# First-block weights of a linear-attention kernel: from a TensorE gram to VectorE row sums, from the second batch on

## The chip, the cores and the metric

The kernel runs on one core of a Trainium2 chip. A core has TensorE (matrix products, with a separate path that loads the stationary operand), VectorE, ScalarE, GpSimd, and SyncE, whose queue issues nearly all DMAs here. In the profile's rows they are PE, PEld, DVE, ACT, POOL and SP. The metric is the device time of one execution in microseconds; shown are medians over several runs, and one further execution is profiled.

## The reference

Two blocks follow each other. The first is a linear attention with a decaying state (B, H, S, D = 4, 8, 768, 48; everything float32); the second is an MLP mixer over tokens and then over channels (model width 384, hidden widths 256 and 1536).

```python
for t in range(S):
    cur = np.einsum('bhd,bhe->bhde', u[None] * kt, vt)
    y[:, :, t] = np.einsum('bhd,bhde->bhe', rt, state + cur)
    state = wt[:, :, :, None] * state + np.einsum('bhd,bhe->bhde', kt, vt)
# x = y with the heads side by side: (B, S, 384)
xt = x.transpose(0, 2, 1)
h = np.maximum(xt @ w_tok1, 0.0) @ w_tok2
u = x + h.transpose(0, 2, 1)
out = u + np.maximum(u @ w_ch1, 0.0) @ w_ch2
```

Written as weights, token t sees an earlier token s with weight sum over d of r[t,d] k[s,d] times the decays w between them. It sees itself with sum over d of r[t,d] u[d] k[t,d], and the token right before it with sum over d of r[t,d] k[t-1,d], with no decay.

## The kernel before

The attention is worked in twelve units: unit i covers 256 tokens of one batch (`NU = 12`, three units to a batch, `UB = 3`), as two chunks of 128 tokens (`UC = 2`) and four pairs of heads (`A = 4`). r, k and w lie with head dimension on partitions and tokens along the row, in three rotating sets of buffers (`rs`, `ks`, `ws`), so unit i uses set i % 3. The weights inside a block of 64 tokens are gathered in `weights_at[i % 3]`, a tile of 128 partitions by 1024.

`levels(i)` makes these weights by doubling block sizes. `begin` (L214) makes on ScalarE two helper copies, `rp` and `kp`, in which r and k of neighbouring tokens are mixed with u, and `first_block` (L325) multiplies the first decays into r and k (`join`, three VectorE products), forms a gram of `kp` and `rp` on TensorE for each chunk (`gram0`, L242, 64 matrix products of the profile's count per unit) and copies the 2 by 2 blocks on the diagonal of it into the weights (`pick0`, L248, two predicated copies on VectorE). Levels 1 to 5 then each run one gram (L265, for level 5 L259), one `join` (L297 to L299) and one `pick` (VectorE's predicated copy L281 for levels 1 to 3, ScalarE copies L276 and L289 for levels 4 and 5). A level's gram reads r and k as the join of the level before left them, and its own join has to wait until the gram has read them.

`post(i)` uses the weights: `tokens` transposes k (L331, copied by ScalarE at L332), `carry` multiplies it with v (L341), `update` advances the state on VectorE (L358, a chain over chunks), `before` multiplies r with the state (L378), `within` multiplies the weights with v (L391), and ScalarE copies the result into x. At its end the loads of unit i + 3 are issued from SyncE.

`mixing(bt)` is the MLP of a batch: `hidden` (L429), `back` (L436, whose result VectorE adds to x at L438), `turn` (transposes L448), `up` (L456, ScalarE applies the relu at L458), and the second channel product, which for all but the first 256 tokens is done in `quarters` as seven half-size products (L490) in place of eight. The seven results are read from PSUM by ScalarE (L499) or VectorE (L500 to L528) and summed; VectorE also makes three sums of z beforehand (L482 to L485). Their PSUM tiles and those of `up`, `hidden` and `back` share two buffers (`ps_m`), so a product can start only when the product two before it has been read. The grams, the transposed k and some `turn`s share two other buffers (`ps_g`).

The order of the work: the attention of batch 0 runs at the start, woven with the conversion of the mixer's weights, which VectorE makes from 64-bit input. From then on `woven` lays the attention pieces of the following batch (units 3 to 5 beside batch 0's mixer, 6 to 8 beside batch 1's, 9 to 11 beside batch 2's) between the pieces of the mixer, by given costs. `beside` couples unit i's `post` with unit i + 1's `levels`, so that two groups of small products stand next to each other. The framework schedules inside these pieces: it decides the final order of each engine's queue from the dependencies and its own estimates, and each queue then runs strictly in that order.

Lines of the profile that matter below: L226 and L230 (rp, kp on ScalarE), L242, L248, L265, L281, L297 to L299, L358, L438, L482 to L485, L490, L500 to L528.

## Time and profile before

| what | value |
|---|---|
| median of 5 runs | 613.35 us (610.61 to 614.23) |
| profiled execution | 614.57 us, of it the span of the trace 612.9 us |
| TensorE matrix products busy | 584.3 us, 95% of the span |
| TensorE weight loads busy | 498.1 us, 81% |
| VectorE busy | 341.2 us, 56% |
| ScalarE busy | 201.6 us, 33% |
| moved by DMA | 38.63 MB, mean 63 GB/s |

A row of the page's groups reads: line, engine, operation, tile written <- tiles read, shapes and count, then the busy time in us, the mean ns of one, and the idle time of the engine just before the group with what ended most of it. The timeline gives start, duration, engine, line, operation and count, with idle time in front in brackets. Matrix products overlap, so a duration is longer than the distance from one start to the next; the same holds to a lesser degree on VectorE (a 0.69 us product is followed by the next start after 0.61 us).

### The profile page before, as it was taken

The numbers are of one execution on the slowest core, as the hardware profiler recorded it, in microseconds if no ns is written. First come the engines' busy times: TensorE is split into PE (matmuls) and PEld (weight loads), VectorE is DVE, ScalarE is ACT, GpSimd is POOL, SyncE is SP. The second block draws the span as 40 slices with busy tenths as digits, with TensorE's granted clock in tenths as the row PEclk, the third lists the DMA queues.
The fourth block names the chain that finished last, engine by engine and source line by source line (L and its number), as shares of the span: only waits on it lengthen the run. The fifth ranks groups of instructions, "written<-read, shape, count | busy, mean of one in ns | idle before, by whom it ended". The sixth has DMA issues, their size and how long they took to land.

```text
span 612.9 us, 19865 instructions
## 1 busy us (share of the span) xinstructions
PE 584.3 (95%) x8980; PEld 498.1 (81%) x8980; DVE 341.2 (56%) x743; ACT 201.6 (33%) x500; POOL 7.2 (1%) x32
## 2 busy tenths in 40 slices
PE   2889789999999999999999999999999999999997
PEld 2777567876988886789899896789899895898987
DVE  5889789998676783636464472516254431040403
ACT  6154555530445433432332422332212411302020
POOL 4000000000000000000000000000000000000000
PEclk9999679999999999999999999999999999999999
DMA  8336564620232212111112100000000000000000
GB/s 346 112 81 215 150 175 157 214 84 27 55 107 80 55 55 79 28 49 32 54 28 79 27 29 27 2 2 3 27 2 28 2 17 11 1 14 14 27 1 26
DMA packets 19380, 38.63 MB, mean 63 GB/s; under 512 B 2112, under 2 KB 12864, under 8 KB 19296
## 3 DMA queue, kind: packets, MB, share of 16 engines
q1 hardware_dynamic: 19152, 37.36, 19.3%
q8 instruction: 70, 1.15, 0.8%
q14 instruction: 14, 0.11, 0.1%
q10 hardware_dynamic: 144, 0.00, 0.0%
HBM read 32.64 MB, written 4.72 MB: 61 GB/s over the span
## 4 chain that ended last, share of the span: by engine, by line
PE 86%; DVE 7%; ACT 3%; issue 2%; DMA 2%; SPq 0%; ACTq 0%; DVEq 0%
PE z_ps L456 28%; PE q_ps L490 24%; PE gram L265 8%; PE h_ps L429 6%; PE h_ps L436 5%; PE h_ps L466 3%; PE y_ps L391 2%; PE kv_ps L341 2%; PE gram L331 2%; PE y_ps L378 2%; PE xT_ps L448 1%; PE gram L242 1%; PE gram L259 1%; DMA scratch<-in_w_ch_dram 1%; DVE state L358 1%
## 5 line engine op out<-in xcount | busy, mean ns | idle before, releaser
L456 PE MATMUL z_ps<-xT,wch 128*128 128x256 f32 x864 | 196.1, 382 | 0.1
L456 PEld LDWEIGHTS z_ps<-xT,wch 128*128 128x128 f32 x864 | 160.9, 190 | 22.1 <-ACT z L458 1.0
L458 ACT ACTIVATE z<-z_ps 128x256 f32<-128x256 f32 x144 | 55.0, 382 | 149.3 <-PE z_ps L456 140.3
L490 PE MATMUL q_ps<-wch,z 128*128 128x192 f32 x528 | 94.8, 329 | 0.0
L490 PEld LDWEIGHTS q_ps<-wch,z 128*128 128x128 f32 x528 | 86.1, 190 | 1.4
L265 PEld LDWEIGHTS gram<-r,k 48*64 48x64 f32 x3072 | 60.5, 156 | 12.6 <-issue 7.2
L490 PE MATMUL q_ps<-scratch,z 128*128 128x192 f32 x396 | 70.6, 329 | 0.0
L265 PE MATMUL gram<-r,k 48*64 48x32 f32 x3072 | 65.6, 237 | 4.7 <-issue 1.9
L490 PEld LDWEIGHTS q_ps<-scratch,z 128*128 128x128 f32 x396 | 64.4, 190 | 0.5
L297 DVE TENSOR_TENSOR k<-k,decay 112x512 f32<-112x512 f32 x36 | 24.8, 690 | 47.3 <-PE gram L265 35.4
L482 DVE TENSOR_TENSOR z<-z 128x768 f32<-128x768 f32 x11 | 10.5, 957 | 60.4 <-ACT z L458 60.4
L297 DVE TENSOR_TENSOR k<-k,w 112x512 f32<-112x512 f32 x36 | 24.8, 689 | 34.6 <-PE gram L265 29.0
L358 DVE SCALAR_TENSOR_TENSOR state<-state,w_chunk,kv_ps 128x48 f32<-128x48 f32 x160 | 30.8, 257 | 21.2 <-PE kv_ps L341 21.1
L429 PE MATMUL h_ps<-x,wtok 128*128 128x384 f32 x96 | 39.8, 562 | 1.7 <-ACT x L397 1.6
L436 PE MATMUL h_ps<-h,wtok 128*128 128x384 f32 x96 | 35.5, 493 | 0.1
L438 DVE TENSOR_TENSOR x<-x,h_ps 128x384 f32<-128x384 f32 x24 | 13.3, 554 | 36.6 <-PE h_ps L436 36.1
L281 DVE COPY_PREDICATED at<-mask,gram 128x512 f32<-128x512 uint8 x36 | 32.3, 898 | 0.0
L429 PEld LDWEIGHTS h_ps<-x,wtok 128*128 128x128 f32 x96 | 19.9, 219 | 13.2 <-issue 3.0
L289 ACT COPY at<-gram 16x256 f32<-16x256 f32 x48 | 17.4, 363 | 38.6 <-PE gram L265 37.4
L242 PE MATMUL gram<-rp,kp 48*64 48x64 f32 x768 | 18.0, 245 | 10.9 <-ACT kp L230 7.9
L298 DVE TENSOR_TENSOR r<-r,w 112x512 f32<-112x512 f32 x36 | 24.6, 685 | 4.8 <-ACT rp L226 4.8
L242 PEld LDWEIGHTS gram<-rp,kp 48*64 48x64 f32 x768 | 15.9, 154 | 12.7 <-ACT kp L230 10.7
(77 smaller groups left out, 554.5 us busy)
## 6 DMA issues: line engine op xcount, KB each, us to landing
scratch<-in_w_ch_dram SPq DMA_DIRECT2D x10, 512.0 KB, 4.5
vt<-in_v_dram SPq DMA_DIRECT2D x12, 384.0 KB, 3.5
out_dram<-o SPq DMA_DIRECT2D x24, 192.0 KB, 1.9
x<-in_w_ch_dram SPq DMA_DIRECT2D x8, 512.0 KB, 4.5
w<-in_rkw_dram SPq DMA_DIRECT2D x18, 192.0 KB, 3.6
k<-in_rkw_dram SPq DMA_DIRECT2D x18, 192.0 KB, 3.1
r<-in_rkw_dram SPq DMA_DIRECT2D x18, 192.0 KB, 3.7
scratch<-in_w_tok_dram SPq DMA_DIRECT2D x4, 512.0 KB, 9.1
```

Of the source, the lines that this page charges most:

```text
L242: pe.matmul(g[cols, q, ts(a, T)], L["kp"][rows, tokens], L["rp"][rows, tokens], start=True, stop=True)
L265: fours(lambda q, j, rows, cols: pe.matmul(g[cols, q, ts(ca, 32)], k_[rows, ds(ca * 128 + j * T, T)], right[rows, ts(2 * ca + j, 32 // b), ...
L281: dve.copy_predicated(out=dst, data=g.rearrange("p q (m b) -> p q m b", b=b), mask=masks[l].rearrange("p x t -> p (x t)").rearrange("p (m ...
L297: dve.tensor_mul(left, left, wv[:, :, 1].unsqueeze(2).to_broadcast([ROWS, n, b]))
L298: dve.tensor_mul(right, right, wv[:, :, 0].unsqueeze(2).to_broadcast([ROWS, n, b]))
L358: dve.scalar_tensor_tensor(new[:, a], state[bt, g][:, a], L["w"][:, c, a, j:j + 1], got[:, a], op0=ALU.mult, op1=ALU.add)
L429: pe.matmul(sums[i], wtok1[:, c, ts(i, 128)], xs[bt][:, c, :], start=(c == 0), stop=(c == C - 1))
L436: pe.matmul(ps, wtok2[:, i, ts(c, 128)], h1[:, i, :], start=(i == 0), stop=(i == DTOK // 128 - 1))
L456: pe.matmul(ps, wch1[:, m, ts(jt, 128)], xT[:, m, ts(s, SEG)], start=(m == 0), stop=(m == DM // 128 - 1))
L458: act.activation(zs[s][:, jt, :], ps, AF.Relu)
L466: pe.matmul(ps, zs[0][:, jt, ts(n, 128)], wch2[:, jt, :], start=(jt == 0), stop=(jt == NJ - 1))
L490: pe.matmul(ps, a[:, j, :], b[:, j, :], start=(j == 0), stop=(j == HJ - 1))
```

## The change

For units 3 to 11 the helper copies `rp`, `kp`, the grams `gram0` and the picks `pick0` are gone, and `begin` does the first `join` alone. The weights of the first block size come from another form of the input: `near`, laid out by the host with tokens on partitions, holds for each token its r, the r of the token after it (zero for odd tokens) and its k, 384 numbers each; `u_all` is u, the same on all 128 partitions. For each unit and chunk VectorE multiplies the two rows of r with k, multiplies the first product with u, and sums each over the 48 numbers of a head (`row`). `place` puts the two sums of each head into a small tile of pairs (four instructions on 8 numbers per partition) and writes them into the weights with one predicated copy of 1024 numbers per partition, repeated along the row under the mask. Four DMAs per unit bring the rows into the pool buffers that had the names `rp` and `kp`; they are issued from SyncE right after `place` of the unit before, and for unit 3 after the last weight conversion has been issued, together with `u_all`. `late` keeps the SyncE and VectorE instructions of unit 3's rows behind what was recorded on those two engines before them. In `beside` the pieces move up: `carry` now stands with the gram of level 1, `before` with level 2 and `within` with level 3; `row` and `place` of the unit after stand between.

```diff
+    def newest(engine):
+        return next(ins.name for ins in reversed(block.instructions) if ins.engine == engine.engine)
+    def late(marks, f):
+        done = len(block.instructions)
+        f()
+        for ins in block.instructions[done:]:
+            for engine, mark in marks.items():
+                if ins.engine == engine.engine:
+                    tc.add_manual_dep(ins, mark, no_sync, reason="order of issue")
...
+            odd = const.tile([128, 1], f32, name="odd")
+            dve.tensor_reduce(out=odd, in_=m[:, :, 0], axis=mybir.AxisListType.X, op=ALU.add)
+            dve.tensor_scalar(odd, odd, -1.0, 1.0, op0=ALU.mult, op1=ALU.add)
...
@@ levels, begin
+            if i >= UB:
+                join(0, products[0], products[1])
+                return
...
-        pieces = [(0.1, begin), (1.6, first_block)]
+        pieces = [(0.1, begin)] + ([(1.6, first_block)] if i < UB else [])
...
+    def load_near(i):
+        if i >= NU:
+            return
+        L = near_by[i] = [apool.tile([128, COLS], f32, name="kp", bufs=1)]
+        for c in range(UC):
+            t = apool.tile([128, COLS], f32, name="rp")
+            sp.dma_start(t[:, :2 * DM].rearrange("p (two e) -> p two e", two=2), near[i - UB, c, :, :2, :])
+            sp.dma_start(L[0][:, ts(c, DM)], near[i - UB, c, :, 2, :])
+            L.append(t)
...
+        def row(c):
+            k, t = near_by[i][0][:, ts(c, DM)], near_by[i][1 + c]
+            rr = t[:, :2 * DM].rearrange("p (two e) -> p two e", two=2)
...
+            dve.tensor_mul(rr, rr, k.unsqueeze(1).to_broadcast([128, 2, DM]))
+            dve.tensor_mul(rr[:, 0], rr[:, 0], u_rows)
+            dve.tensor_reduce(out=sums[0][:, c], in_=t[:, :2 * DM].rearrange("p (h e) -> p h e", e=D),
+                              axis=mybir.AxisListType.X, op=ALU.add)
+        def place():
+            own, later = (sums[0][:, :, ts(n, H)].rearrange("p c (a q) -> p q c a", q=2) for n in range(2))
+            two = apool.tile([128, 2, UC * A, 2], f32, name="two")
+            v = two.rearrange("p q (c a) two -> p q c a two", c=UC)
+            for q in range(2):
+                dve.tensor_copy(v[:, q, :, :, 0], own[:, q])
+                dve.scalar_tensor_tensor(v[:, q, :, :, 1], own[:, q], odd, later[:, q], op0=ALU.mult, op1=ALU.add)
+            dve.copy_predicated(
+                out=weights_at[i % 3].rearrange("p q x (m two) -> p (q x) m two", two=2),
+                data=two.rearrange("p q x two -> p (q x) two").unsqueeze(2).to_broadcast([128, 2 * UC * A, T // 2, 2]),
+                mask=masks[0].rearrange("p x (m two) -> p x m two", two=2).to_broadcast([128, 2 * UC * A, T // 2, 2]))
+        return [(0.3, lambda: row(0)), (0.3, lambda: row(1)), (0.2, lambda: (place(), load_near(i + 1)))]
...
@@ beside
-        return [(1.0, begin[1]), tokens, one(carry, first), update, one(before, rest[0]), one(within, rest[1]),
-                *loads, *rest[2:]]
+        return [(1.0, begin[1]), tokens, one(carry, rest[0]), update, one(before, rest[1]), row0, one(within, rest[2]),
+                *loads, row1, *rest[3:], place]
...
@@ the loop over batches
-            att = levels(n) if bt == 0 else []
+            att = []
+            if bt == 0:
+                marks = {e: newest(e) for e in (sp, dve)}
+                late(marks, lambda: (sp.dma_start(u_rows, u_all), load_near(n)))
+                att += levels(n) + [(c, lambda f=f: late(marks, f)) for c, f in nearest(n)]
             for i in range(n, n + UB):
-                att += beside(post(i), levels(i + 1)) if i + 1 < NU else post(i)
+                att += beside(i, post(i), levels(i + 1)) if i + 1 < NU else post(i)
...
@@ kernel, on the host
+    following[:, 0::2] = r[:, 1::2]
+        "near": np.stack([r, following, k], axis=2).reshape(NU - UB, UC, 128, 3, DM),
+        "u_all": np.broadcast_to(inputs["u"].reshape(1, DM), (128, DM)),
```

## The prediction, made before the changed kernel had run

> **What bounds the kernel now.** I read the page's busy times first, then the busy time by stretches, then what TensorE waits for, then the timelines of TensorE and VectorE around one unit.

> ```profile
> PE 584.3 (95%) x8980; PEld 498.1 (81%) x8980; DVE 341.2 (56%) x743; ACT 201.6 (33%) x500; POOL 7.2 (1%) x32
> ...
> PEclk9999679999999999999999999999999999999999
> ```
> ```profile
> 134.00:235.00 101.00, 99.25 (x2272) 82.50 (x2271) 76.57 (x163) 36.30 (x95) 0.34 (x3) 1.00 0.23 65
> 235.00:243.00 8.00, 8.00 (x38) 4.55 (x40) 0.03 (x1) 2.16 (x4) 0.00 (x0) 1.00 0.20 51
> 243.00:456.00 213.00, 211.76 (x3376) 183.67 (x3375) 104.83 (x236) 66.40 (x171) 0.23 (x2) 1.00 0.10 28
> ```
> ```profile
> PE xT_ps L448 <- DVE at L248: 0.8, 1, 0.8
> PE gram L265 <- DVE r L298: 0.4, 1, 0.4
> ```

> The columns of the stretches are stretch, length, then busy time and count of PE, PEld, DVE, ACT and POOL, the granted clock and the DMA share. From 134 us on TensorE is never without work for more than a few tenths: 99.25 of 101 us and 211.76 of 213 us, at clock 1.00. The two waits shown are all that the wait list names on PE between 243 us and the end. So a product taken off TensorE there shortens the run, provided nobody else becomes late. VectorE is the one to watch: it is busy 76.6 of 101 us in the first stretch (units 3 to 6, beside batch 0's mixer) but only 104.8 of 213 us in the second (units 7 to 11).

> Timeline of TensorE around unit 5's first gram, and of VectorE a little later:

> ```profile
> 175.08 1.13 PE L265 MATMUL gram<-r,k 48*64 48x32 f32 x64
> 176.14 1.99 PE L456 MATMUL z_ps<-xT,wch 128*128 128x256 f32 x8
> 178.06 1.14 PE L265 MATMUL gram<-r,k 48*64 48x32 f32 x64
> 179.13 1.99 PE L456 MATMUL z_ps<-xT,wch 128*128 128x256 f32 x8
> ...
> 186.16 1.15 PE L341 MATMUL kv_ps<-vt,kT 64*64 64x48 f32 x64
> 187.13 1.13 PE L242 MATMUL gram<-rp,kp 48*64 48x64 f32 x64
> ```
> ```profile
> 188.26 0.73 DVE L248 COPY_PREDICATED at<-mask,gram 128x512 f32<-128x512 uint8 x1
> 188.88 0.42 DVE L358 SCALAR_TENSOR_TENSOR state<-state,w_chunk,kv_ps 128x48 f32<-128x48 f32 x2
> ...
> 194.98 1.33 DVE L281 COPY_PREDICATED at<-mask,gram 128x512 f32<-128x512 uint8 x1
> 196.08 0.35 DVE L299 TENSOR_TENSOR decay<-w 112x128 f32<-112x128 f32 x1
> ...
> 203.60 0.17 DVE L299 TENSOR_TENSOR w_chunk<-decay 112x16 f32<-112x16 f32 x1
> ...
> 209.52 0.95 DVE L484 TENSOR_TENSOR z<-z,z 128x768 f32<-128x768 f32 x1
> 210.39 0.95 DVE L485 TENSOR_TENSOR z<-z 128x768 f32<-128x768 f32 x1
> ```

> Read distances from start to start, since durations overlap. A gram takes 1.06 us of TensorE (175.08 to 176.14). VectorE's price is 0.62 us for a predicated copy of 512 numbers (188.26 to 188.88), but 1.10 for the one that writes pairs of numbers (194.98 to 196.08), and 0.87 for a product of 768 (209.52 to 210.39).

> **What is removed from TensorE.** Nine units lose a gram, 9 x 1.06 = 9.5 us. Each also loses one change between large and small products, because the grams move up: with carry, before and within stand levels 1, 2 and 3, and two grams stand alone instead of three. Eight z products between two grams take 1.92 us (176.14 to 178.06); in an unbroken run of 30 (299.76 to 306.43) one takes 0.222, so eight would take 1.78 and the edges cost 0.14. With 18 products between grams (261.86 to 265.94, 4.08 us) they cost 0.08. I take 0.07 us, so 1.13 us a unit and 10.2 us in all. ScalarE loses two copies (0.67 us) and eight scalings (0.40) a unit, 4.5 us; it is busy a third of the time and I cost that at nothing, as the waits on it vanish only where PE waited (none from 134 us on). POOL is as it was.

> [...] The starts in the timeline, one group directly behind the other, say that the engine has no free slots, so I keep the full figure.

> **What is added to VectorE.** A chunk's row is a product of 768 (0.87), one of 384 (L438, 0.55 long, 0.47 to the next start) and a sum of 768 into 16. The trace has no sum along a row; its bounds are 0.44 (a one-source tensor_scalar of 512 numbers, L180, goes on after 0.34, scaled by size) and 1.65 (the pair-writing copy's 1.10 for 512, scaled). I take 0.86, that of the other 768-number rows. Row: 2.20, two rows 4.4 a unit. Place: four instructions on 8 numbers, 0.13 each (the L299 row of 16 numbers, 0.17 long), 0.5; and a predicated copy of 1024 numbers that reads pairs repeatedly but writes one dense run: between 2 x 0.60 = 1.2 and 2 x 1.10 = 2.2. I take 1.25, because L248 writes densely and costs 0.62, and what is slow in L281 is the form that writes pairs. Sum 6.2 us a unit, less two pick0 (1.24): about +4.9, or 44 us over nine units. [...]

> **Where this lies.** The built program's order on VectorE decides, and it is not spread evenly. Between the last weight conversion (134 us in the run before) and the first addition of L438 in batch 1 (243 us) stand the rows of seven units, 3 to 9: the scheduler pulls them ahead as soon as their loads may be in. So that stretch gets 14 rows (30.8 us), four large placements (5.0) and six sets of small ones (3.0), and loses six pick0 (3.7) and unit 3's level 1 (2.5, now before 134 us, which starts the stretch 1.3 us later). Net +32.6 us, against 109 - 76.6 = 32.4 us of idle time. VectorE fills up completely, and becomes the bound there. Adding the start distances one by one from 135.4 us, the join that unit 6's level-5 gram waits for ends at 232.9 us; before, that gram began at 231.87. So in this stretch TensorE saves four grams (4.5 us) and loses them and 1 us more in waits of 0.4 to 2.3 us each: the grams of levels 3 to 5 wait for L298's successor, the products with the state wait for L358. I add 0.5 us for rows whose next instruction needs their result (L482 to L483: 0.99 instead of 0.87). Stretch one: +1.5 us.

> From 243 us on there are left two units' rows (8.8 us), five placements and five pick0 less, against 108 us of idle VectorE time: hidden by the long runs of z and q products. TensorE saves five grams, 5.7 us. The wait of xT_ps for L248 (0.8) should mostly go, as a unit now takes one gram buffer less; the placements stand before readings of q_ps and may cost some tenths in places. Stretch two: -6.0 us.

> Before 134 us unit 3's gram of level 1 takes the place of its first gram, behind the same k and v product; VectorE's 1.3 us delay falls beside 30 us of z products. Nothing.

> **DMA and SyncE.** Nine times four loads, 1.2 MB a unit, plus u_all (0.2 MB). The share was 0.23 and below; a load of near is 0.2 or 0.4 MB, and the rkw loads (192 KB) land in 3.1 to 3.7 us, vt's (384 KB) in 3.5, so I take 3.5. SyncE issues in order: a load of near waits for the sum of two rows before it, and loads of r, k, w, v and the stores of the output stand behind it. In the stretch each row's load may start 6 to 20 us before its use by the sums above, so nothing waits; r, k, w are needed a unit later (20 us or more). If a load comes late, VectorE waits at the head of its queue, and with it all joins. At unit 11's second row (about 260 us) I expect such a wait of some 2 us, beside z products.

> **The sum.** Profiled execution: span 612.9 + 1.5 - 6.0 = 608.4, with the 1.7 us around it 610.1 us. The median of the runs lies 1.2 us under that execution: 608.9 us.

> **Rivals.**
> 1. VectorE's additions stay hidden in the first stretch as well. For it: the sums may cost 0.44 instead of 0.86, 13 x 0.42 = 5.5 us less before the gram in question. Against it: two-source work of 768 numbers has 0.87. Then 10.2 + 0.8 = 11 us go: 602.4 us.
> 2. Slower: the row sum at up to 1.65 us in the first stretch. 13 sums x 0.79 = 10.3 us more on an engine with no idle time left, all of it paid: 608.9 + 10.3 = 619.2. It ends above 613.35 from 0.34 us more for each sum, that is 1.2 us. The placement at 2.2 alone (3 x 0.95 = 2.9 us) gives 611.8. Against it: products with broadcast and pair patterns (L297) run at full rate in every shape shown.
> 3. SyncE's queue: near's loads stand behind loads of k and r that wait for TensorE, or share the DMA engines with them. One wait of a load's 3.5 us in the full stretch is paid in full, and one more can follow: 612 to 616 us. For it: one queue for everything; against it the distances above.
> 4. The change gives TensorE nothing, since the next grams only move closer and wait for their joins everywhere: 613 us. The 108 us of idle VectorE time after 243 us speak against it.

> **How the numbers follow.** 0.5% of 613 us, 3 us, is about what a measurement of this kernel can tell from no change. Forecast 0.50 (own range 606 to 612), rival 1 0.16, rival 2 with a price that counts 0.18, rival 3 0.11, rival 4 0.05. Faster by over 3 us: 0.42 of the forecast's 0.50 and all of rival 1, 0.58. Slower: most of rival 2 and a little of 3, 0.18. Same: the rest, 0.24. The range leaves out the fastest tenth and the slowest: 603 to 617.

> **What would show it.** Right: L242's successor with 192 products instead of 768, VectorE busy nearly all of 134 to 235 us, TensorE waits there on joins and state, about 5 us in sum, and few after 243 us; VectorE about 385 us busy, ScalarE about 160. Wrong: a row sum or placement far from 0.86 or 1.25; VectorE waiting for DMA between 134 and 235 us; idle time of VectorE left in that stretch; new TensorE waits after 243 us.

## The result and the profile after

The changed kernel takes 612.84 us in the median of 36 executions (608.49 to 615.84); the kernel before takes 613.5 (71 executions, 610.59 to 616.28). The ratio is 0.9987, with an interval of 0.9976 to 0.9999. The forecast was 608.9 us, a ratio of 0.993. The gain in the median is 0.7 us instead of 4.5. The executions of the changed kernel spread over more than 7 us, and the one that was profiled first lies near the lower end: 609.53 us, of it the span 607.7. A reader of that one profile would think that the forecast (span 608.4) had come true.

The page's busy times and granted clock, answering to the first fence of before:

```profile
PE 569.9 (94%) x8404; PEld 486.3 (80%) x8404; DVE 380.1 (63%) x826; ACT 169.0 (28%) x410; POOL 7.2 (1%) x32
...
PEclk9997669999999999999999999999999999999999
```

The same three stretches, in the same columns:

```profile
134.00:235.00 101.00, 92.12 (x1976) 76.96 (x1975) 97.96 (x210) 23.61 (x60) 0.34 (x3) 1.00 0.43 122
235.00:243.00 8.00, 8.00 (x93) 5.21 (x74) 7.93 (x15) 3.12 (x7) 0.00 (x0) 1.00 0.62 190
243.00:456.00 213.00, 212.84 (x3150) 184.80 (x3149) 116.25 (x261) 54.56 (x137) 0.23 (x2) 1.00 0.14 40
```

VectorE is busy 97.96 of 101 us and TensorE 92.12 instead of 99.25: the first stretch has become VectorE's, as forecast. In the second TensorE has no idle time left to speak of. What TensorE waits for, over the whole run (releaser, us in total, times, longest):

```profile
PE gram L289 <- issue: 6.7, 7, 2.3
PE y_ps L445 <- DVE state L425: 4.3, 5, 1.4
PE gram L289 <- DVE r L322: 3.7, 4, 1.5
...
PE xT_ps L515 <- DVE x L505: 0.2, 1, 0.2
```

Two of these were forecast: the joins (L322, L298 before) and the state (L425). The first was not. "Issue" is time in which the profile shows nothing that the engine waited for. It was 1.9 us for grams before and is 6.7 now; of it 3.4 us lie between 134 and 243 us, in two stops.

The longest wait for a join between 134 and 243 us has a cause of its own, a load of r that came late. SyncE had stood 8.7 us at a load of `near` until the buffer came free; the load of r stood behind it:

```profile
SPq L348 <- DVE rp L362: 8.7, 1, 8.7
```
```profile
193.85 1.89 SPq L348 DMA_DIRECT2D kp<-in_near_dram  x2
195.83 0.85 SPq L128 DMA_DIRECT2D r<-in_rkw_dram  x2
```
```profile
200.45 0.69 DVE L322 TENSOR_TENSOR r<-r,w 112x512 f32<-112x512 f32 x1 [1.48 <-DMA r<-in_rkw_dram]
```
```profile
202.49 1.13 PE L289 MATMUL gram<-r,k 48*64 48x32 f32 x62 [1.47 <-DVE r L322]
204.63 0.30 PE L289 MATMUL gram<-r,k 48*64 48x32 f32 x2 [1.01 <-issue]
```

VectorE stood 1.48 us for r at the head of its queue, and TensorE 1.47 us for the join behind it; the first of the two stops by issue follows 1.1 us later. In the kernel before, the same load was issued at 192.83 us, as soon as the state's product had read the buffer, the product of r began at 199.22, and VectorE waited for no load between 134 and 243 us. In all six profiles of the changed kernel it waits there for r, by 0.4 to 1.9 us.

The new work on VectorE, by form (count, busy time, mean ns of one):

```profile
L362 DVE TENSOR_TENSOR rp<-rp,kp 128x768 f32<-128x768 f32 x18 | 17.1, 951 | 1.3 <-DMA rp<-in_near_dram 1.2
L364 DVE TENSOR_REDUCE sums<-rp 128x16 f32<-128x768 f32 x18 | 16.9, 944 | 0.1
L375 DVE COPY_PREDICATED at<-mask,two 128x1024 f32<-128x1024 uint8 x9 | 11.8, 1309 | 1.0 <-ACT at L300 0.9
```

From start to start the sum is 0.86 to 0.87 us and the placement 1.20 us: the two prices that the trace of before did not have were 0.86 and 1.25 in the forecast.

Three points of TensorE's work cut the run into three parts that can be compared between executions: the first product of h_ps with z (L466 before, L533 after; about 133 us) and the first product of `back` in batch 1 (L436, L503; about 243 us). For the kernel before, and for six profiled executions of the changed one (five of them taken later, see the experiments):

| execution, us | start | stretch one | from there to the end | clock, 134 to 243 us |
|---|---|---|---|---|
| before, 614.57 | 133.5 | 107.7 | 371.6 | 1.00 |
| after, 607.41 | 131.2 | 110.3 | 364.0 | 1.00 |
| after, 609.53 | 132.9 | 110.7 | 364.1 | 1.00 |
| after, 611.06 | 134.4 | 110.8 | 364.0 | 1.00 |
| after, 612.27 | 133.7 | 112.7 | 364.0 | 0.97 |
| after, 613.56 | 133.8 | 113.9 | 364.0 | 0.95 |
| after, 614.37 | 133.8 | 114.6 | 364.1 | 0.95 |

The last part is 7.5 to 7.6 us shorter in every one of them. Stretch one is longer by 2.6 to 3.1 us in three, and by 5.0 to 6.9 in the others, which are the ones where TensorE was granted less than its full clock. The start varies by 3 us on its own account: of the 7.0 us between the fastest and the slowest of the six, 4.3 lie in stretch one and 2.6 in the start. In the kernel before and four variants of it that leave stretch one as it was, stretch one takes 107.0 to 108.6 us.

### The profile page after: what moved, and what is told of

Read it like the earlier page. It is cut to its first block, busy times and chain, and to the rows that moved or that the text cites. A ratio compares the mean times of both kernels' runs of the same rounds, so it can differ in the third digit from the quotient of the medians.

```text
span 607.7 us, 18750 instructions
## 1 busy us (share of the span) xinstructions
PE 569.9 (94%) x8404; PEld 486.3 (80%) x8404; DVE 380.1 (63%) x826; ACT 169.0 (28%) x410; POOL 7.2 (1%) x32
## 4 chain that ended last, share of the span: by engine, by line
PE 72%; DVE 19%; issue 4%; ACT 2%; DMA 2%; SPq 0%; DVEq 0%; ACTq 0%
PE z_ps L523 24%; PE q_ps L557 22%; PE gram L289 6%; PE h_ps L496 6%; PE h_ps L503 5%; PE y_ps L458 2%; DVE r L322 2%; PE y_ps L445 2%; DVE state L425 2%; PE kv_ps L408 2%; DVE k L321 2%; DVE at L305 1%; DVE wch L205 1%; PE gram L398 1%; PE xT_ps L515 1%
## 5 line engine op out<-in xcount | busy, mean ns | idle before, releaser
L425 DVE SCALAR_TENSOR_TENSOR state<-state,w_chunk,kv_ps 128x48 f32<-128x48 f32 x160 | 30.2, 256 | 16.3 <-PE kv_ps L408 16.2
L503 PE MATMUL h_ps<-h,wtok 128*128 128x384 f32 x96 | 35.3, 492 | 0.0
L322 DVE TENSOR_TENSOR r<-r,w 112x512 f32<-112x512 f32 x36 | 24.6, 684 | 3.9 <-DMA r<-in_rkw_dram 3.9
L322 DVE TENSOR_TENSOR r<-r,decay 112x512 f32<-112x512 f32 x36 | 24.6, 684 | 0.0
L503 PEld LDWEIGHTS h_ps<-h,wtok 128*128 128x128 f32 x96 | 16.6, 190 | 9.6 <-ACT h L498 2.6
```

The lines of the kernel that those rows point to most:

```text
L322: dve.tensor_mul(right, right, wv[:, :, 0].unsqueeze(2).to_broadcast([ROWS, n, b]))
L425: dve.scalar_tensor_tensor(new[:, a], state[bt, g][:, a], L["w"][:, c, a, j:j + 1], got[:, a], op0=ALU.mult, op1=ALU.add)
L503: pe.matmul(ps, wtok2[:, i, ts(c, 128)], h1[:, i, :], start=(i == 0), stop=(i == DTOK // 128 - 1))
```

## The experiments

Ratios are to runs of the kernel before on the same chip. The theories: **A**, VectorE is full and TensorE waits for its place in VectorE's order; **B**, what varies lies ahead of 134 us; **C**, loads of `near` hold up others, in SyncE's queue or on the DMA engines; **D**, behind a long stop TensorE gets half its clock; **E**, TensorE's own instructions come late. D and E were formed on the way.

### The changed kernel again, and its parts

**The changed kernel unchanged.**

> The changed kernel once more, for a second profile. Its median over many runs lay 0.7 us below the kernel before, its first profile 5.2 us below in the span. Theory A (VectorE is full between 134 and 235 us and TensorE waits there): median 612 to 613.5 us, TensorE without work for 8 to 12 us of that stretch, under 1 us between 243 and 456 us. Theory B (what varies lies ahead of 134 us, in loads and the granted clock of the start): the stretch and what follows take the same as in the first profile within 1 us, and the start of the last conversion's end moves by the difference in the total. Theory C (loads that come late while VectorE has no idle time left): a profile with a longer span has more waits of VectorE for DMA in that stretch than the 1.5 us of the first.

Measured: 610.91 us (609.09 to 612.92, 9 executions), ratio 0.9949 (0.9929 to 0.9968); none of the nine above 613. A's median was missed. Between the two profiles B's forecast held: stretch one took 110.7 and 110.8 us, and the difference of 1.5 us lies in the start (132.9 and 134.4). VectorE's waits for loads in stretch one were 2.2 us in the longer one, as C expected, at no cost that shows. The interval does not meet that of the first 36 executions (0.9976 to 0.9999): the changed kernel differs by some 2 us from one set to the next, and a gain of that size over it has to be read with care.

**Rows and placement held back on VectorE** until the pieces before them are issued, so that the scheduler cannot pull them ahead (and the loads of `near`, which wait for their buffers, come later too).

> Each unit's row sums and placement are kept behind the VectorE work recorded before them, so that only units 3 to 6 have theirs ahead of batch 1's first addition to x, instead of units 3 to 9; nothing else differs. Theory A: VectorE busy about 88 of 101 us in 134 to 235 us, TensorE's missing work there falls from 9 to about 4 us, time 607 to 609 us. Theory B: the start is that of the changed kernel, so 612 to 613 us. Theory C: fewer loads compete in the stretch and VectorE can make up a late one, 608 to 610 us.

```diff
-        row0, row1, place = nearest(i + 1)
+        row0, row1, place = ((c, lambda f=f: late({dve: newest(dve)}, f)) for c, f in nearest(i + 1))
```

Measured: 606.05 us (604.89 to 608.11, 6 executions), ratio 0.9873 (0.9847 to 0.9898). Its first stretch:

```profile
134.00:235.00 101.00, 97.07 (x2020) 80.67 (x2019) 92.83 (x198) 25.93 (x66) 0.34 (x3) 0.98 0.39 112
```

VectorE has idle time again and TensorE stands 3.9 us in stretch one, where it was 8.9 in the changed kernel and 1.8 before. Nothing but the order of the same work, and with it the times of the loads, is different. This beats both kernels: stretch one takes 106.9 us. TensorE's waits there for joins and state fell to 1.8 us, VectorE waits for no load any more, and 1.9 us of stops by issue are left. So the gain was beyond A's 607 to 609, and it is not all VectorE's order: the late load of r is gone with it.

**The new form from unit 7 on only**, with the loads of the first rows at the start of batch 1.

> The new form for units 7 to 11 only; units 3 to 6 keep their first gram, and the start and batch 0's mixer are as in the kernel before. Theory A: five grams and some 1 us of waits less, nothing lost: 606 to 608 us. Theory B: the same, since the start is that of the kernel before. Theory C: 606 to 609 us, TensorE's missing work in 134 to 235 us as in the kernel before, 1.8 us. If the gram's price is not what TensorE gets back, 610 us or more.

```diff
-            if i >= UB:
+            if i >= FIRST:          # FIRST = 7
...
-        pieces = [(0.1, begin)] + ([(1.6, first_block)] if i < UB else [])
+        pieces = [(0.1, begin)] + ([(1.6, first_block)] if i < FIRST else [])
```

Measured: 614.7 us (612.96 to 617.47, 12 executions), ratio 1.0023 (1.0004 to 1.0041). A expected 606 to 608 and is wrong here. The cost has moved with the rows. Between 243 and 291 us VectorE is busy 41.63 of 48 us, because the scheduler now gathers the rows of the remaining units there, and TensorE stands. Timeline of TensorE:

```profile
284.65 0.60 PE L399 MATMUL gram<-ident,k 128*128 128x128 f32 x4
288.69 1.51 PE L558 MATMUL q_ps<-scratch,z 128*128 128x192 f32 x6 [3.44 <-DVE o L572]
```

The reading of q_ps (o, L572) stood behind a placement (282.76), one product of decays and four sums of z. So it is not the place of the stretch that costs: five units' rows gathered between 236 and 291 us cost as well. The gathering is not shown to be the whole cause, since loads of `near` came late too. VectorE stood for them five times between 233 and 280 us, for 8.9 us in all (releaser `kp`; `rp` is another 2.0):

```profile
DVE rp L363 <- DMA kp<-in_near_dram: 6.9, 3, 2.7
```

And behind the stops at 248.8 us (2.29 us) and 288.7 the clock was at half for 3.4 us each.

**The work of the rows left out, their loads kept.**

> The row products and sums are left out (one product of 16 numbers stands in for each chunk's row, so the weights of the first block size are wrong); loads, placements and the missing grams stay. Theory A: VectorE has idle time in 134 to 235 us again, TensorE's missing work there is 2 to 4 us, and nearly the whole price of the grams comes back: 602 to 605 us. Theory B: the loss ahead of 134 us stays: 606 to 608 us. Theory C: late loads still stop VectorE but it can make them up: 603 to 605 us.

```diff
-            dve.tensor_mul(rr, rr, k.unsqueeze(1).to_broadcast([128, 2, DM]))
-            dve.tensor_mul(rr[:, 0], rr[:, 0], u_rows)
-            dve.tensor_reduce(out=sums[0][:, c], ...)
+            dve.tensor_mul(sums[0][:, c], t[:, :2 * H], k[:, :2 * H])
```

Measured: 612.17 us (606.02 to 615.49, 12 executions), ratio 0.9962 (0.9936 to 0.9988). VectorE is busy only 76.26 of the 101 us, as before the change, and TensorE still stands for 6.8 us of stretch one. All three expectations were missed. So VectorE's fullness is not the whole cause. With the rows' work gone their buffers come free at once, the loads of `near` are issued earlier and closer together, and a row of 16 numbers whose load is late holds the head of VectorE's queue:

```profile
153.70 0.18 DVE L362 TENSOR_TENSOR sums<-rp,kp 128x16 f32<-128x16 f32 x1 [1.88 <-DMA kp<-in_near_dram]
153.79 0.68 DVE L321 TENSOR_TENSOR k<-k,w 112x512 f32<-112x512 f32 x1
154.39 0.68 DVE L322 TENSOR_TENSOR r<-r,w 112x512 f32<-112x512 f32 x1
```

The gram behind that join stood 2.17 us. VectorE waited for r as well, 4.7 us in two waits. Another stop, 2.62 us at 226.5, is put down to issue, while the DMA engines were busy all the time (share 0.92 to 1.06 from 221 to 227 us). Behind each of the two the clock was about 0.5 for some 3 us.

**The loads of `near` left out, the work kept** on one block of numbers.

> The changed kernel, but the rows of all units are computed from one block of numbers that is loaded once, so the weights of the first block are those of other tokens: no load of near is left in SyncE's queue or on the DMA engines, and VectorE's work is the same. Theory A (VectorE is full between 134 and 235 us, TensorE waits for its place in VectorE's order): 608 to 613 us like the changed kernel, TensorE idle for 7 to 9 us between 133 and 243 us, VectorE busy for over 96 of the 101 us from 134 to 235. Theory C (loads of near hold up the loads of r, k and w): 604 to 607 us, TensorE idle there for less than 4 us.

```diff
-            sp.dma_start(t[:, :2 * DM]..., near[i - UB, c, :, :2, :])
-            sp.dma_start(L[0][:, ts(c, DM)], near[i - UB, c, :, 2, :])
+        # once, for unit 3; every row then reads the same tile
...
-            dve.tensor_mul(rr, rr, k.unsqueeze(1).to_broadcast([128, 2, DM]))
+            dve.tensor_mul(rr, same[:, :2 * DM]..., same[:, COLS - DM:]...)
```

Measured: 607.39 us (606.84 to 608.08, 4 executions), ratio 0.9902 (0.9873 to 0.993).

```profile
134.00:235.00 101.00, 95.11 (x2015) 78.44 (x2014) 101.00 (x215) 25.00 (x64) 0.34 (x3) 1.00 0.23 64
```

VectorE is busier than in the changed kernel, all of the 101 us, and yet TensorE stands less. Most of the waits for joins and state remains (2.8 and 1.2 us, against 3.7 and 1.6); VectorE's wait for r is gone, the time put down to issue shrinks from 3.4 to 1.2 us between 134 and 243 us, and the clock is 1.00. So the loads cost some 3 us (ratios 0.9949 and 0.9902, whose intervals just meet), more against the first 36 executions (0.9987), and not by filling VectorE. The time lies between the two forecasts, and both theories had a part.

**The loads of `near` on another queue**, added to the version that holds the rows back.

> The version that holds rows and placement back on VectorE (606.05 us), with the loads of near issued from GpSimd's queue instead of SyncE's, so that no load of r, k, w or v stands behind one that waits for its buffer; the orders on TensorE, VectorE and ScalarE are the same. Theory A (what is left of the loss is VectorE's order): 605 to 607 us, as before the move. Theory C (loads of r come late behind loads of near): 602.5 to 604.5 us, with TensorE idle for less than 2.5 us between 133 and 239 us, where it was 3.9.

```diff
-            sp.dma_start(t[:, :2 * DM]..., near[i - UB, c, :, :2, :])
-            sp.dma_start(L[0][:, ts(c, DM)], near[i - UB, c, :, 2, :])
+            pool.dma_start(t[:, :2 * DM]..., near[i - UB, c, :, :2, :])
+            pool.dma_start(L[0][:, ts(c, DM)], near[i - UB, c, :, 2, :])
```

Measured: 605.83 us (605.23 to 608.03, 6 executions), the same as 606.05. TensorE's stops in stretch one went from 3.9 to 3.6 us. In this version SyncE's order, rival 3's mechanism, costs nothing that shows; but VectorE waited for no load in stretch one here before the move either, so the run says nothing on the changed kernel, where it did. (The first loads now ran at 16 and 43 us, beside the loads of the weights, and the profiled start was 135.3 us; whether that took back a gain is open.)

### How much VectorE work is free after 300 us

> The kernel before, with 6, 8, 10 and 14 idle products of 384 numbers put on VectorE between the two joins of level 4 of units 8, 9, 10 and 11 (0.47 us each by the trace), so that the gram of level 5 comes late by about 2.4, 3.4, 4.3 and 6.2 us: four stops of TensorE with nothing else changed. Theory D (behind a stop of some 2 us or more TensorE gets only half its clock for 3 to 4 us, in some executions and not in others, which costs 1.7 us more than the stop): the granted clock falls to about 0.5 behind at least two of the four, and the time is that of the kernel before, 613.9, plus the stops (up to 16 us) plus 3.4 to 7 us. Without D: the granted clock stays 1.00 behind all stops, and the time grows by no more than the stops themselves.

```diff
+            if (i, l) in STOPS:     # {(8, 4): 6, (9, 4): 8, (10, 4): 10, (11, 4): 14}
+                for _ in range(STOPS[i, l]):
+                    late({dve: newest(dve)}, lambda: dve.tensor_mul(ones, ones, ones))
+                late({dve: newest(dve)}, lambda: dve.tensor_mul(right, right, ...))
```

Measured: 614.25 us (612.0 to 617.18, 10 executions), ratio 1.0012 (0.9988 to 1.0035). The products ran, and TensorE's waits from 300 us on:

```profile
L316 DVE TENSOR_TENSOR ones<-ones x38: 550/558/560, 318.6 to 484.1; 128x384 f32<-128x384 f32 x38
```
```profile
PE xT_ps L470 <- DVE at L264: 0.8, 1, 0.8
PE gram L275 <- DVE r L317: 0.4, 1, 0.4
PE gram L281 <- DVE r L320: 0.4, 1, 0.4
```

The attempt to stop TensorE failed, so it decides nothing on theory D, and tells something else: 38 products, 17.9 us of VectorE time put in bunches of 2.8 to 6.6 us between two joins, cost nothing that can be measured. That the scheduler puts z and q products where the late gram would have stood is my reading of it. It fits the second part of the forecast, that the rows of two units and the placements after 243 us are hidden; the rows of five units were not.

### What "issue" is

In the trace without loads TensorE's timeline reads:

```profile
221.76 0.65 PE L557 MATMUL q_ps<-scratch,z 128*128 128x192 f32 x3 [0.16 <-issue]
222.34 1.15 PE L458 MATMUL y_ps<-vt,at 64*64 64x48 f32 x64
223.31 1.09 PE L289 MATMUL gram<-r,k 48*64 48x32 f32 x61
225.37 0.30 PE L289 MATMUL gram<-r,k 48*64 48x32 f32 x3 [0.98 <-issue]
```

From one stop to the next are 3 + 64 + 61 = 128 products, and the second falls into the middle of a gram, where the profile shows nothing to wait for. Each product has its weight load (8980 of each on the page of before), so that is 256 instructions. In the changed kernel the same gram is cut at the same product:

```profile
224.18 1.15 PE L458 MATMUL y_ps<-vt,at 64*64 64x48 f32 x64
225.14 1.09 PE L289 MATMUL gram<-r,k 48*64 48x32 f32 x61
228.58 0.30 PE L289 MATMUL gram<-r,k 48*64 48x32 f32 x3 [2.35 <-issue]
```

The DMA answers list a queue of its own for instructions. In the half microsecond from 226.0, 2.1 to 2.6 us before TensorE went on, it moved one packet of 0.02 MB (packets, MB, share of 16 engines):

```profile
q1 hardware_dynamic: 11, 0.01, 25.3%
q8 instruction: 1, 0.02, 11.8%
```

So the reading is that the instructions come in pages of 256, over the same DMA engines, and that TensorE stands when it has used up a page (here 128 products in 2.1 us, from 224.1) before the next is there. The count fits: in the kernel before, this queue moved 70 packets of 16 KB, 1.15 MB, and 70 times 256 is 17920, for 2 x 8980 products and weight loads. In that kernel the packet of the page that a gram at 226.26 waited for came between 223.5 and 224.0, again 2.3 to 2.8 us ahead; but the 128 products of the page in use had lasted 4.2 us (221.84 to 226.08), and the stop was 0.18 us. So 128 small products in a row made a stop even without loads of `near` (0.98 us above), and with the loads it was longer (2.35). To test this I put idle products ahead of everything, where TensorE waits for its first loads (until 7.91 us in the kernel before); they move every page bound by 52 products (the profile counts the 26 as 52, from 2.05 us on), and but for a few neighbours the order of all other instructions in the trace is the same.

> The changed kernel with 26 idle products put ahead of everything on TensorE, where it waits for its first loads anyway; the order of all other instructions on all engines is the same. Theory E: TensorE's instructions arrive in pages of 128 products by a transfer of their own on the same DMA engines, and where 128 products run within some 2.6 us and loads of near are under way, the next page comes late; this is the idle time that the profile puts down to issue (1.0 us at 204.6 and 2.35 at 228.6, always 128 products or a multiple apart). The 26 products move the page bounds by 52 products, out of the dense places: these two stops shrink to less than 1 us in sum, the half clock behind the longer one goes, and the median is 607 to 609.5. Theory A alone (VectorE's order makes the stops): nothing changes, 610 to 613, with stops at the same products. Theory C alone (late loads of r): nothing changes either.

```diff
+    for _ in range(2):
+        idle = ps_m.tile([128, DM], f32, name="idle_ps", tag="m")
+        for j in range(13):
+            pe.matmul(idle[:64, :8], weights_at[0][:, 0, 0, :], weights_at[0][:, 0, 0, :8], start=True, stop=True)
```

Measured: 608.7 us (607.65 to 612.92, 9 executions), ratio 0.9932 (0.9911 to 0.9953). What TensorE waits for from 131 to 250 us:

```profile
PE gram L294 <- DVE r L327: 4.9, 5, 1.8
PE y_ps L450 <- DVE state L430: 1.4, 3, 0.6
PE gram L403 <- DVE k L326: 1.0, 1, 1.0
```

No stop is put down to issue any more, and the clock is 1.00. Part of what goes comes back as waits for joins (7.3 us on joins and state, against 5.3 in the first profile), since VectorE is still full and still waits 1.0 us for r; stretch one of the profiled execution takes 108.5 us instead of 110.3 at the least. The time is as E forecast, and the stops are gone as forecast. The gain over the changed kernel is clear against the first 36 executions, not against the nine of the later set (0.9949, 0.9929 to 0.9968). The control is the kernel before with the same 26 products:

> The kernel before, with the same 26 idle products ahead on TensorE; all other orders are the same. It tells whether the idle products help by themselves. Theory E (the page bounds matter where loads of near delay the page): the kernel before has only 0.8 us of stops put down to issue from 134 us on, so at most that goes: 612.5 to 614. If the idle products help by something else, a warm start of TensorE for instance, it falls by 2 to 4 us as the changed kernel did: 609.5 to 611.5.

Measured: 613.57 us (611.66 to 614.83, 12 executions), ratio 0.9988 (0.9969 to 1.0007). The idle products do nothing that shows by themselves. And with the version that holds rows back:

> The version that holds rows and placement back on VectorE (606.05 us), with the same 26 idle products ahead. Theory E: its stops put down to issue (0.4 us at 218.0 and 1.5 at 222.1) and the half clock behind them (1.6 us) go, and nothing takes their place: 602.5 to 604.5. Otherwise 605 to 607.

Measured: 605.12 us (604.92 to 605.84, 4 executions), ratio 0.9863 (0.9848 to 0.9878). The expectation of 602.5 to 604.5 was missed. Stretch one fell from 106.9 to 104.8 us in the profiles, but the start took 134.2 us instead of 131.8, and against 606.05 the gain is not clear. It has the lowest median here; the version without the idle products and the one with the loads on GpSimd's queue lie within 1 us of it.

### The spread between executions: half clock behind a stop

A second profile of the changed kernel, and then three more to catch one of over 613 us.

> The changed kernel unchanged, for a second profile beside that of the first one. Its runs fall into 608 to 612 and 613 to 616 us. Theory D: if this one takes over 613 us, the granted clock falls to about 0.5 behind one or two stops of TensorE between 190 and 235 us; if it takes less than 611, the clock stays at 1.00 there. Theory B (what varies lies ahead of 134 us): the first product h_ps of the channel mixing comes at another time than 132.9 us by as much as the time differs, and the rest is the same.

> The changed kernel again, to catch in a profile one of its executions of over 613 us (two of five of the first 36, none of nine later). Theories D and E together: such an execution has the clock at half behind two or more places between 60 and 240 us and stops put down to issue of more than 3.4 us in sum between 134 and 243 us, while the gain after 243 us is the same 7 us as in the others. Theory B: the stretch from 134 to 243 us is as in the first profile (110.7 us) and the start is 2 to 4 us later. An execution below 611 us has no half clock between 134 and 243 us.

> The changed kernel once more: over 613 us goes with half clock and stops by issue of over 3.4 us between 134 and 243 us (D and E) or with a start 2 to 4 us later alone (B); below 611 us with neither of them.

> The changed kernel a last time: over 613 us goes with half clock and stops by issue of over 3.4 us between 134 and 243 us (D and E) or with a start 2 to 4 us later alone (B); below 611 us with neither of them.

They took 612.27, 607.41, 613.56 and 614.37 us (single executions); the table above has their parts. TensorE's stops between 134 and 250 us are nearly the same in the fastest and the slowest: 3.7 us on joins, 1.5 on the state and 3.2 put down to issue at 607.41, and 3.8, 1.5 and 3.2 at 614.37. So the expected "over 3.4 us by issue" did not show, and neither did a later start alone; what differs in stretch one is the granted clock, the last column but two, of the stretches behind the stops. The execution of 614.37 us:

```profile
201.67:205.08 3.41, 1.79 (x66) 1.38 (x64) 3.08 (x6) 0.38 (x1) 0.00 (x0) 1.00 0.71 259
205.08:211.90 6.82, 5.71 (x81) 4.21 (x77) 4.62 (x9) 2.45 (x7) 0.00 (x0) 0.50 0.42 98
...
228.97:232.38 3.41, 1.34 (x54) 1.19 (x47) 3.41 (x9) 1.30 (x3) 0.00 (x0) 1.00 0.54 175
232.38:235.79 3.41, 3.41 (x13) 3.41 (x12) 1.80 (x3) 0.00 (x0) 0.00 (x0) 0.50 0.40 120
```

And the one of 607.41, in the same places of the program:

```profile
197.68:201.09 3.41, 1.91 (x21) 1.38 (x20) 2.21 (x4) 0.38 (x1) 0.00 (x0) 1.00 0.93 329
201.09:204.50 3.41, 2.57 (x70) 2.28 (x66) 3.12 (x8) 1.24 (x4) 0.00 (x0) 1.00 0.02 5
221.57:224.98 3.41, 2.59 (x129) 2.25 (x127) 3.41 (x12) 1.42 (x3) 0.00 (x0) 1.00 0.61 179
224.98:228.39 3.41, 1.88 (x13) 1.84 (x14) 3.16 (x7) 0.00 (x0) 0.00 (x0) 1.00 0.32 102
```

Behind the pair of stops near 204 us (1.6 and 1.1 us there, 1.5 and 0.8 here; the first of each pair is the one behind the late load of r) and behind the one near 230 (2.1 and 2.4) the clock went to half, for 6.8 and 3.4 us, in the one and not in the other. Both dips came at 613.56 too, only the later one at 612.27, none in the three below 611.1. By the table one dip goes with about 2 us more in stretch one, two with 3 to 4.

The limits of these stretches are points where the clock changed, or lie whole steps of 3.41 us from one. In all 17 traces the changes lie whole multiples of 3.41 us apart, at other points of the program in each execution. From 134 us to 20 us before the end, every step of 3.41 us at full clock in which TensorE was busy for at most 0.39 of it was followed by half clock (nine steps); of those busy for 0.49 to 0.56 four were and seven were not; above that none was. So in these executions a stop counted by how much of one step it took: at 614.37 the stop of 2.07 us fell into one step (busy 1.34 of 3.41 us); at 607.41 the longer one of 2.35 us was shared by two (2.59 and 1.88), and nothing followed.

To see which stops do it by themselves, the kernel before got six halts in batch 3's mixer, where TensorE has one stream of products and nothing can be put in the gap.

> The kernel before, with six halts of TensorE put into batch 3's mixer, where nothing but z, q and h products runs: a product, then 1, 3, 4, 9, 4 and 6 idle products of 384 numbers on VectorE (0.47 us each) that need its result, then a product that needs theirs. TensorE should stand for about 1.1, 2, 2.5, 4.8, 2.5 and 3.4 us, 16.3 us in all. Theory D: behind the halts of over 3 us the granted clock is about 0.5 for some 4 us, behind 1.1 us it stays 1.00, behind 2 to 2.5 us it is one or the other; each time costs 1.7 to 2 us, and the time is 613.3 plus 16.3 plus 3.5 to 10 us, 633 to 640. Without D: the clock is 1.00 behind all of them and the time 629 to 631.

```diff
+    def stop(n):
+        ps, ps2 = (ps_m.tile([128, DM], f32, name="idle_ps", tag="m") for _ in range(2))
+        pe.matmul(ps[:64, :8], ident[:, :64], ident[:, :8], start=True, stop=True)
+        dve.tensor_copy(ones[:64, :8], ps[:64, :8])
+        for _ in range(n):
+            dve.tensor_mul(ones, ones, ones)
+        pe.matmul(ps2[:64, :8], ones[:, :64], ones[:, :8], start=True, stop=True)
```

Measured: 647.82 us (644.57 to 649.74, 4 executions), ratio 1.0556 (1.0518 to 1.0594). Three of the halts:

```profile
543.08 0.28 PE L583 MATMUL idle_ps<-ones 128*64 128x8 f32 x2 [3.52 <-DVE ones L582]
...
561.78 0.28 PE L583 MATMUL idle_ps<-ones 128*64 128x8 f32 x2 [2.68 <-DVE ones L582]
...
578.41 0.38 PE L583 MATMUL idle_ps<-ones 128*64 128x8 f32 x2 [5.59 <-DVE ones L582]
```

and the stretches behind them:

```profile
542.00:546.00 4.00, 2.92 (x12) 2.90 (x13) 2.76 (x4) 0.00 (x0) 0.00 (x0) 0.71 0.02 4
...
562.00:566.00 4.00, 4.00 (x20) 3.54 (x20) 0.00 (x0) 0.77 (x2) 0.00 (x0) 1.00 0.00 2
578.00:582.00 4.00, 3.58 (x10) 2.94 (x11) 0.36 (x1) 0.25 (x1) 0.00 (x0) 0.50 0.02 4
582.00:586.00 4.00, 4.00 (x14) 3.31 (x13) 0.00 (x0) 0.64 (x3) 0.00 (x0) 0.67 0.00 0
```

Behind the halts of 3.52, 3.81 and 5.59 us the clock fell to half (twelve q products took 3.87 us instead of 2.1); behind 0.84 and twice 2.68 it stayed at 1.00. The step of 3.41 us ahead of the fall was busy for 0.18, 0.36 and 0.00 of it. The halts sum to 19.1 us and the profiled time, 644.57, is 31 above the kernel before: these stops cost more than their length, and behind these halts the DMA engines were all but idle (share 0.02 and less). Some 13 us of TensorE's work ran at half clock, 6.5 us more by estimate; the remaining 5 are not explained, and the expectation of 633 to 640 was missed.

## Why the prediction was wrong

- **What is removed from TensorE: right in kind, 1.6 us too small after 243 us.** From 243 us to 456 TensorE is 0.16 us idle of 213, and the part to the end is 7.6 us shorter, forecast 6.0. The wait of xT_ps shrank from 0.8 to 0.2 us as expected; idle time from 243 to 456 us fell by 1.1 us in all. The rest of the surplus was not traced.
- **What is added to VectorE: right**, price by price (0.86 for the sum, 1.20 for 1.25). The eight-number instructions were 0.07 and 0.14 us apart, 0.42 us for four, a little under the forecast's 0.5. Rival 2 had no ground. Rival 1's low bound for the sum was misworked (0.34 us for 512 numbers, scaled by size, is 0.51 and not 0.44), which changes nothing, as the sum took 0.86. ScalarE was busy 169.0 us, forecast about 160; no wait came of it.
- **VectorE full from 134 to 235 us: right in place and size.** The rows, four large placements and six sets of small ones stand there as forecast (13 sums instead of 14). TensorE's waits on joins and state are 5.3 us there, forecast about 5, but 1.5 of them come from the late load of r. Holding the rows back left 1.8.
- **"Stretch one: +1.5 us" is the step that failed.** It summed VectorE's starts and priced TensorE's stops by their length, with full clock behind them. With the clock undisturbed it is +2.6 to +3.1: the waits on joins and state, 4.6 us more than before, are about the 4.5 us of grams saved, and what stands over is two stops that were not in the sum, pages of instructions that come late where the loads of `near` use the DMA engines (3.4 us there, 0.8 before). And in three of the six profiled executions the stops bring half clock, another 2 to 4 us, which is +5.0 to +6.9 in all. The forecast looked only at busy time and waits of a trace in which no stop after 134 us was longer than 0.8 us, so that it showed neither.
- **DMA: "nothing waits" failed with it.** It asked which data each load delays and took r, k and w to be needed 20 us after their loads. The trace of before already showed less: r issued at 192.83 us, used at 199.22. With SyncE held up by `near`, VectorE was at r's first product before the load had landed in every profile (0.4 to 1.9 us). The other late transfer, the pages of instructions, was none of the kernel's own. The wait for `near` of some 2 us, forecast at about 260, came at 263.8 with 1.2.
- **The sum.** For the profiled execution it comes out right by chance: 3.0 too much and 7.6 off instead of 1.5 and 6.0 give 608.3, forecast 608.4; two errors cancel. "The median lies 1.2 us under that execution" was carried over from before to after, and that was wrong: the first profile after is one without half clock and lies 3.3 us under the median.
- **Rival 3** named the right range, 612 to 616 us, with loads of `near` as the cause, by waits for k and r. That wait is in the trace, but it is 0.4 to 1.9 us of the loss and not 3.5 or more; the late pages and the half clock, which make up the rest, are not in the rival. Moving the loads to another queue gained nothing in a version without the wait; taking them away gained some 3 us. **Rival 4's** 613 us is the median too, by luck: TensorE did gain the 7.6 us behind 243 us that it denied.

Open: why none of nine executions in a later set exceeded 613 us when two of five of the first 36 did; how much of the loss the late load of r makes by itself, and the late page by itself, since in the changed kernel they stand next to each other; and what makes the start vary by 3 us.

## What to carry to other kernels

Work that the bound engine shed was worth its full time here only where the other engine had room: two units' rows were hidden after 243 us and seven cost more than they saved ahead of it, and one line that keeps the scheduler from bunching them gained 4.9 us on the changed kernel (610.91 to 606.05). Stops of 1.5 to 2.6 us on TensorE brought half clock in some executions, which cost about 2 us a dip above their length, and one profile was not enough to see it: where a change opens such stops, compare the granted clock behind the stops in several executions. SyncE's queue stood 8.7 us at a load whose buffer was not free, and the load of r behind it came 1.48 us late: look at what the next load in a queue is for. Where a stop is put down to issue, count the products between two of them (128 or a multiple here) before looking for a semaphore.
